# Attention key tiles: the odd 64 keys of two head pairs in one tile, and two pairs' sums in one PSUM bank

## The chip, the cores and the metric

One Trainium2 chip, one core. The metric is the device time of one execution in microseconds. The kernel before took 1009.11 us, the median of three runs (1012.57, 1009.09, 1009.11). One more execution, of 1010.09 us, was profiled.

## What is computed

Three layers in one kernel, all fp32. The change touches only the first.

```
# 1. random-feature attention: q, k, v of (4 batches, 8 heads, 576 positions, 64)
phi(x) = exp(h - max(h)) / sqrt(128),  h = x @ omega.T - sum(x*x)/2       # 128 features
kv  = sum over keys of phi(k)^T v        # (b, h, 128, 64)
z   = sum over keys of phi(k)            # (b, h, 128)
out = (phi(q) @ kv) / (phi(q) @ z + 1e-6)
# 2. x: (2304 tokens, 512) -> RMS norm -> silu(x w_gate) * (x w_val) -> w_out, d_ff 1536
# 3. 8 experts, capacity 288 each, greedy assignment by logits, relu(x w1) w2
```

576 keys are four tiles of 128 and a rest of 64.

## The kernel before, in words

**Layout.** The host lays k out as `kT[b, p]`, for pair p of heads (four pairs): 128 partitions are two heads by 64 dimensions, and 640 columns are the keys, the last 64 of them zero. `v1[b, p]` holds, for each of five tiles of 128 keys, both heads' values with a column of ones behind them (65 columns), zero where there is no key. The column of ones makes z come out with kv.

**Items.** Attention is a list of items. A `KItem(b, p, g)` takes key tiles 2g and 2g+1 of a pair; g = 2 has tile 4 only. A `QItem(b, t, hf)` takes 128 or 64 query rows and half of the heads. Per batch there are 12 key items and 10 query items, 88 in all. The loop over `tick` runs a new item in each tick, with six stages ("lags") of items overlapping.

A key item in lag 0 projects its tiles onto the features (for batch 0 by one fp32 matmul per tile, line 371; for the others by three fp32r matmuls of split operands, lines 366 to 368), takes the negated maximum (DVE, line 375) and two exponentials per tile (ACT, line 378). In lag 1 it multiplies the features with the values into a PSUM tile `pm` (line 412), which collects a pair's sums over its five tiles; after the last, ACT copies the 130 columns into `kvs` (line 422). For batches 1 to 3 the keys are split ahead of that (ACT line 341, GpSimd line 342). An fp32 matmul leaves two rows in the trace.

PSUM: `pm` has three banks, shared by the sums over keys and by three tiles of a query item; `pp` (projections) two, `gv` (feed-forward) two, `lg` one.

**Loads.** `load_k` (lines 332 and 333) is called three items ahead of a pair's first key item, on SP's queue, into tiles `kt` and `vt` of two buffers each; batch 0 is loaded at the start into rooms of another pool. SP's queue also carries the weights (line 518), queries (353) and stores (612).

**What runs beside attention.** Weights of layer 2 come as 64-bit words; 36 conversion units (24 of w_gate and w_val, 12 of w_out) turn them into fp32 with an ACT operation and three of DVE each (lines 526 to 528). They start at a rate of 0.3 per tick up to tick `FFN_AT` = 23, then two per tick until the first 24 are out, then 0.5 per tick. Feed-forward steps (24 fp32r matmuls each, lines 595 to 597, then ACT and DVE, lines 606 to 620) run one per tick, two in the dense ticks, as soon as a block of 256 tokens and its weights are there; from the third block on a step also waits for a unit of w_out. When a query item needs a fourth block, steps are run in a burst until one is free. Attention's instructions are traced with a raised priority (`AHEAD_A`), and a scheduler orders each engine's queue by priority and readiness. Behind attention, the rest of the feed-forward steps, the second half of layer 2 with the routing (a hand-written order) and the experts follow.

The start flag clears a whole bank's accumulation state, so only the first matmul into a `pm` tile sets it:

```
pk = st["pk", b, p]
for i, t in enumerate(self.ts):
    for h in range(2):
        nc.tensor.matmul(pk[:, h * (D + 1):(h + 1) * (D + 1)], self.ft[:, 2 * i + h, :], vt[:, t, h, :],
                         start=(t == 0 and h == 0), stop=(t == 4), skip_group_check=True)
```

Of the kernel before, what the change touches and what calls it, by code (L numbers as in the profile page):

```python
# [9 lines left out]
F32 = mybir.dt.float32  # L10
# [9 lines left out]
B, H, S, D, M = 4, 8, 576, 64, 128  # L20
# [21 lines left out]
EARLY = 6  # L42
SUB = 1
PACE = (0.3, 1.0, 0.5)
FFN_AT = 23
AHEAD_A = 200
HB = 6
LATE = 2
# [5 lines left out]
def const_f32():  # L54
    c = np.zeros((128, C_N), np.float32)
    i = np.arange(128)
    c[:, C_ID:C_SL] = np.eye(128)
    c[:, C_SL:C_SA] = np.arange(SL)
    c[:, C_SA:C_C] = np.arange(NSL)
    c[:, C_C:C_P] = np.arange(NC)  # L60
    c[:, C_P] = i
    c[:, C_E:C_T] = np.arange(E)
    e = np.arange(E)
    c[:, C_T:C_N] = (e[None, :] < e[:, None]).reshape(-1)
    return c


def triangles():
    i = np.arange(128)
    j = np.tile(np.arange(CAP), (128, 1))  # L70
    return np.concatenate([i[:, None] < i[None, :], i[:, None] >= i[None, :], j], 1).astype(np.float32)


def const_i32():
    rows = []
    for n, (d, s) in enumerate(zip(DIGITS, SHIFTS)):
        j = np.arange(1 if n else 2, 1 << d, dtype=np.uint32) << np.uint32(s)
        if n == 0:
            j = np.where(j >= 0x80000000, j ^ np.uint32(0x80000000), ~j)
        rows.append(j.astype(np.uint32))  # L80
    return np.tile(np.concatenate(rows).view(np.int32), (128, 1))
# [198 lines left out]
def kernel(ctx, tc, qT, kT, v1, om, wgv, rms, wo, wg2, w1, w2, cfd, trd, cid, out, dbg=None):  # L280
    nc = tc.nc
# [31 lines left out]
    kq = ac.enter_context(tc.tile_pool(name="kq", bufs=2))  # L313
    at = ac.enter_context(tc.tile_pool(name="at", bufs=2))
    psA = ac.enter_context(tc.tile_pool(name="psA", bufs=1, space=PSUM))

    st = {}


    kts, vts, khs, kvs, qhs = {}, {}, {}, {}, {}  # L320
    xblk, ready = {}, []

    def load_k(b, p):
        if b == 0:

            room = wpool.tile([128, 2, 1024], F32, name="wc")
            kt = room[:, 0, :640]
            vt = room[:, 1, :10 * (D + 1)].rearrange("p (t h d) -> p t h d", t=5, h=2)
        else:
            kt = kq.tile([128, 640], F32, name="kt")  # L330
            vt = kq.tile([128, 5, 2, D + 1], F32, name="vt")
        nc.sync.dma_start(kt, kT[b, p])
        nc.sync.dma_start(vt, v1[b, p])
        kts[b, p], vts[b, p] = kt, vt

    def split_k(b, p, g):
# [28 lines left out]
    def proj(pp, xh, xl):  # L365
        nc.tensor.matmul(pp, xh, omh, start=True, stop=False)
        nc.tensor.matmul(pp, xh, oml, start=False, stop=False)
        nc.tensor.matmul(pp, xl, omh, start=False, stop=True)  # L368

    def proj_whole(pp, x):  # L370
        nc.tensor.matmul(pp, x, oms, start=True, stop=True)

    def feat(pp, n, ng):
        mx = at.tile([128, 4], F32, name="mx")
        nc.vector.tensor_reduce(out=mx[:n, :ng], in_=pp[:n, :ng], axis=AX.X, op=OP.max, negate=True)  # L375
        ft = at.tile([128, 4, M], F32, name="ft", bufs=3)
        for g in range(ng):
            nc.scalar.activation(ft[:n, g], pp[:n, g], AF.Exp, bias=mx[:n, g:g + 1])  # L378
        return ft

    class KItem:
        def __init__(self, b, p, g):
            self.b, self.p, self.g = b, p, g
            self.ts = [t for t in (2 * g, 2 * g + 1) if t < 5]

        def load(self):
            if self.g == 0 and self.b:
                load_k(self.b, self.p)
# [5 lines left out]
        def pe(self, lag):  # L394
            b, p, g = self.b, self.p, self.g
            if lag == 0:
                self.pp = psA.tile([128, 4, M], F32, name="pp", bufs=2)
                if b == 0:
                    for i, t in enumerate(self.ts):
                        proj_whole(self.pp[:, 2 * i:2 * i + 2, :], kts[b, p][:, t * 128:t * 128 + 128])  # L400
                    return
                kh, kl = khs.pop((b, p, g))
                for i, t in enumerate(self.ts):
                    proj(self.pp[:, 2 * i:2 * i + 2, :], kh[:, i * 128:i * 128 + 128], kl[:, i * 128:i * 128 + 128])
            elif lag == 1:
                if g == 0:
                    st["pk", b, p] = psA.tile([128, 512], F32, name="pm", bufs=3)
                pk = st["pk", b, p]
                vt = vts[b, p]
                for i, t in enumerate(self.ts):  # L410
                    for h in range(2):
                        nc.tensor.matmul(pk[:, h * (D + 1):(h + 1) * (D + 1)], self.ft[:, 2 * i + h, :], vt[:, t, h, :],  # L412
                                         start=(t == 0 and h == 0), stop=(t == 4), skip_group_check=True)

        def el(self, lag):
            b, p, g = self.b, self.p, self.g
            if lag == 0:
                self.ft = feat(self.pp, 128, 2 * len(self.ts))
            elif lag == 1 and g == 2:
                if p == 0:  # L420
                    kvs[b] = at.tile([128, H, D + 1], F32, name="kvs")
                nc.scalar.copy(kvs[b][:, 2 * p:2 * p + 2, :].rearrange("p h d -> p (h d)"),
                               st.pop(("pk", b, p))[:, :2 * (D + 1)])

    class QItem:
        def __init__(self, b, t, hf):
# [262 lines left out]
    def ffn_step_el():  # L689
        if "el" in fst:  # L690
            j, f, pg = fst.pop("el")
            ffn_el(j, f, pg)
            ffn_rank_el()
            return j, f
        return None


    items = []
    for b in range(B):
        items += [KItem(b, p, g) for p in range(4) for g in range(3)]  # L700
        items += [QItem(b, t, hf) for t in range(5) for hf in range(2)]
    useq = [WgvUnit(f, g) for f in range(KF) for g in range(2)] + [WoUnit(f) for f in range(KF)]
    AHEAD = 3
# [1 line left out]
    ws = stage.tile([128, 2 * M], F32, name="ws")  # L705
    nc.scalar.dma_start(ws, om)
    load_k(0, 0)
    oms = wpool.tile([128, 2 * M], F32, name="wc")
    nc.scalar.mul(oms, ws, SCALE)
# [20 lines left out]
    def conv_pe(pace):  # L730
        conv["due"] += pace
        conv["live"] = [(lag + 1, u) for lag, u in conv["live"] if lag < 3]
        while conv["due"] >= 1 and conv["next"] < len(useq):
            conv["due"] -= 1
            conv["live"].append((0, useq[conv["next"]]))
            conv["next"] += 1
        for lag, u in conv["live"]:
            u.pe(lag)
# [8 lines left out]
    for tick in range(len(items) + NLAG - 1):  # L747
        live = [(lag, items[tick - lag]) for lag in range(NLAG) if 0 <= tick - lag < len(items)]
        conv_pe(PACE[0] if tick < FFN_AT else PACE[1] if conv["next"] < 2 * KF else PACE[2])
        with tc.high_priority(offset=AHEAD_A):  # L750
# [18 lines left out]
        ffn_step_el()  # L769
        if tick >= FFN_AT and conv["next"] < 2 * KF:  # L770
            for r in range(SUB):
# [268 lines left out]
def layouts(q, k, v, omega, moe_w_gate, moe_w_val, moe_w_out, moe_rms_g, moe2_w_gate, moe2_w1, moe2_w2):  # L1040
    a = np.asarray
    hp = H // 2

    def bits(x):
        return np.ascontiguousarray(x).view(np.int64)

    qT = a(q).reshape(B, hp, 2, S, D).transpose(0, 2, 4, 1, 3).reshape(B, 128, hp, S)
    kT = np.zeros((B, hp, 128, 640), np.float32)
    kT[..., :S] = a(k).reshape(B, hp, 2, S, D).transpose(0, 1, 2, 4, 3).reshape(B, hp, 128, S)
    v1 = np.zeros((B, hp, 2, 640, D + 1), np.float32)  # L1050
    v1[:, :, :, :S, :D] = a(v).reshape(B, hp, 2, S, D)
    v1[:, :, :, :S, D] = 1.0
    v1 = v1.reshape(B, hp, 2, 5, 128, D + 1).transpose(0, 1, 4, 3, 2, 5)
    om = np.zeros((128, 2 * M), np.float32)
    om[:D, :M] = a(omega).T
    om[D:, M:] = a(omega).T
    wgv = np.stack([bits(moe_w_gate), bits(moe_w_val)], 0).reshape(2, KD, 128, KF, 128).transpose(3, 2, 1, 0, 4)
    wgv = wgv.reshape(KF, 128, 1024)
    rms = np.tile(a(moe_rms_g)[None], (128, 1))
    wo = bits(moe_w_out).reshape(KF, 128, DM)  # L1060
    wg2 = a(moe2_w_gate).reshape(KD, 128, E).transpose(1, 0, 2)
    w1 = a(moe2_w1).reshape(E, KD, 128, 4, 256).transpose(0, 3, 2, 1, 4).reshape(E, 4, 128, 1024)
    w2 = a(moe2_w2).reshape(E, KE, 128, KD, 128).transpose(0, 3, 2, 1, 4).reshape(E, 4, 128, 1024)
    d = dict(qT=qT, kT=kT, v1=v1, om=om, wgv=wgv, rms=rms, wo=wo, wg2=wg2, w1=w1, w2=w2,
             cf=const_f32(), tri=triangles(), ci=const_i32())
    return {n: np.ascontiguousarray(x) for n, x in d.items()}
# [17 lines left out]
```

## Time and profile before

| | us |
|---|---|
| median of three runs | 1009.11 |
| profiled execution | 1010.09 |
| its span in the profile | 1008.2 |
| PE busy | 971.8 |
| weight loads (PEld) busy | 886.8 |
| DVE busy | 534.5 |
| ACT busy | 399.8 |
| POOL (GpSimd) busy | 242.1 |

The span is the time between the first and the last instruction of the profiled execution. Busy time counts overlapping rows once; rows of PE overlap, since a matmul's row holds its latency. PEld rows are the weight loads, which run beside the matmuls. In the slices of the page a digit is the busy share of 25.2 us in tenths,. "idle <- X" names what ended the idle time before an instruction.

### The profile page before, as it was taken

How to read it: one execution, taken by the hardware profiler on the slowest of the kernel's cores; microseconds unless marked ns; L12 is line 12 of the kernel's file. 1: busy time of each engine (PE TensorE's matmuls, PEld its weight loads, DVE VectorE, ACT ScalarE, POOL GpSimd, SP SyncE). 2: the span in 40 equal slices, each digit the busy share in tenths (PEclk: the TensorE clock that was granted, in tenths of full speed). 3: DMA queues.
4: the chain of work that ended last, by engine and by line, in shares of the span. 5: the costliest groups of instructions: out<-in, count | busy, mean ns of one | idle time of the engine just before them, and what ended most of it. 6: DMA issues, size and time to landing. Idle time of an engine off the chain costs nothing.

```text
span 1008.2 us, 19316 instructions
## 1 busy us (share of the span) xinstructions
PE 971.8 (96%) x7649; PEld 886.8 (88%) x7649; DVE 534.5 (53%) x1239; ACT 399.8 (40%) x999; POOL 242.1 (24%) x325
## 2 busy tenths in 40 slices
PE   6998899999999999999999999999997999999996
PEld 5888899989989989999999777777776999999996
DVE  3779956544653344432234465555554656665531
ACT  4985546546654544332233100100003644444420
POOL 1345512233344222322223000000005121222111
PEclk7999999999999999999999999999998999999998
DMA  8436752366544211732224466655536755655400
GB/s 274 158 113 207 222 160 81 127 212 200 178 144 148 102 53 49 202 112 83 83 98 156 138 183 203 189 175 161 158 94 213 246 187 189 199 194 193 150 24 24
DMA packets 112074, 153.32 MB, mean 152 GB/s; under 512 B 8560, under 2 KB 78832, under 8 KB 111984
## 3 DMA queue, kind: packets, MB, share of 16 engines
q1 hardware_dynamic: 108768, 142.52, 43.8%
q0 software_dynamic: 3072, 9.44, 2.9%
q8 instruction: 60, 0.98, 0.4%
q14 instruction: 30, 0.25, 0.1%
q10 hardware_dynamic: 144, 0.13, 0.0%
HBM read 108.03 MB, written 44.04 MB: 151 GB/s over the span
## 4 chain that ended last, share of the span: by engine, by line
PE 77%; issue 9%; DVE 6%; DMA 2%; ACT 2%; POOL 2%; SPq 0%; POOLq 0%; DVEq 0%; ACTq 0%
PE py L880 16%; PE gv L595 10%; PE gv L596 9%; PE gv L597 9%; PE pm L457 3%; PE pm L412 2%; PE cnt L163 2%; PE ph L968 2%; PE py L978 2%; PE ph L970 2%; PE ph L969 2%; PE py L979 2%; PE py L980 2%; DVE dw L527 2%; PE pm L453 2%
## 5 line engine op out<-in xcount | busy, mean ns | idle before, releaser
L595 PE MATMUL gv<-xh,wc 128*128 128x256 f32 x864 | 253.5, 294 | 6.4 <-DVE hp L610 6.0
L596 PE MATMUL gv<-xl,wc 128*128 128x256 f32 x864 | 250.1, 289 | 0.0
L597 PE MATMUL gv<-xh,wc 128*128 128x256 f32 x864 | 249.7, 289 | 0.0
L880 PE MATMUL py<-wc,ht 128*128 128x512 f32 x648 | 175.9, 409 | 0.0
L595 PEld LDWEIGHTS gv<-xh,wc 128*128 128x128 f32 x864 | 165.1, 191 | 10.7 <-DVE hp L610 7.0
L596 PEld LDWEIGHTS gv<-xl,wc 128*128 128x128 f32 x864 | 165.4, 191 | 0.8
L597 PEld LDWEIGHTS gv<-xh,wc 128*128 128x128 f32 x864 | 165.4, 191 | 0.6
L880 PEld LDWEIGHTS py<-wc,ht 128*128 128x128 f32 x648 | 114.4, 188 | 21.9
L607 DVE SCALAR_TENSOR_TENSOR th<-th,gv 128x256 f32<-128x256 f32 x108 | 45.1, 418 | 122.6 <-ACT th L606 122.4
L378 ACT ACTIVATE ft<-pp,mx 128x128 f32<-128x128 f32 (+1 forms) x320 | 93.9, 373 | 25.9 <-DVE mx L375 24.7
L620 POOL TENSOR_TENSOR hp<-h,hp 128x256 fp32r<-128x256 f32 x84 | 65.5, 780 | 156.1 <-ACT hp L619 156.0
L862 DVE TENSOR_TENSOR wc<-ws,wc 128x1024 fp32r<-128x1024 f32 x58 | 70.9, 1224 | 32.7 <-ACT wc L861 32.4
L606 ACT ACTIVATE th<-gv 128x256 f32<-128x256 f32 x108 | 41.5, 384 | 105.3 <-PE gv L597 105.0
L968 PE MATMUL ph<-exh,wc 128*128 128x288 f32 x256 | 78.9, 309 | 0.0
L978 PE MATMUL py<-ehh,wc 128*128 128x288 f32 x256 | 78.0, 305 | 0.0
L970 PE MATMUL ph<-exh,wc 128*128 128x288 f32 x256 | 76.2, 298 | 0.0
L969 PE MATMUL ph<-exl,wc 128*128 128x288 f32 x256 | 76.1, 298 | 0.0
L979 PE MATMUL py<-ehl,wc 128*128 128x288 f32 x256 | 75.9, 297 | 0.0
L980 PE MATMUL py<-ehh,wc 128*128 128x288 f32 x256 | 75.8, 296 | 0.0
L375 DVE TENSOR_REDUCE mx<-pp 128x4 f32<-128x512 f32 (+2 forms) x88 | 55.6, 635 | 33.9 <-PE pp L368 21.1
L889 ACT COPY ws<-py 128x512 f32<-128x512 f32 x18 | 10.6, 586 | 145.8 <-PE py L880 132.2
L861 ACT CAST wc<-ws 128x1024 fp32r<-128x1024 f32 x58 | 61.0, 1051 | 3.1 <-DMA ws<-in_w_dram 3.0
(197 smaller groups left out, 1843.2 us busy)
## 6 DMA issues: line engine op xcount, KB each, us to landing
ws<-in_w_dram SPq DMA_DIRECT2D x64, 512.0 KB, 3.4
ht<-h_dr SPq DMA_DIRECT2D x54, 512.0 KB, 4.2
h_dr<-hp SPq DMA_DIRECT2D x42, 512.0 KB, 2.6
ws<-in_wgv_dram SPq DMA_DIRECT2D x24, 512.0 KB, 4.0
ws<-in_wo_dram SPq DMA_DIRECT2D x12, 512.0 KB, 4.3
h_dr<-dw SPq DMA_DIRECT2D x24, 256.0 KB, 2.1
y_dr<-ws SPq DMA_DIRECT2D x18, 256.0 KB, 4.3
vt<-in_v_dram SPq DMA_DIRECT2D x12, 325.0 KB, 4.0
```

What stands on the lines that cost most here:

```text
L378: nc.scalar.activation(ft[:n, g], pp[:n, g], AF.Exp, bias=mx[:n, g:g + 1])
L595: nc.tensor.matmul(pg[:, v], w[:, 0, k, v], xh[:, k], start=(k == 0), stop=False)
L596: nc.tensor.matmul(pg[:, v], w[:, 0, k, v], xl[:, k], start=False, stop=False)
L597: nc.tensor.matmul(pg[:, v], w[:, 1, k, v], xh[:, k], start=False, stop=(k == KD - 1))
L862: lo.tensor_sub(w[:, 1], sv, w[:, 0])
L880: nc.tensor.matmul(py, ht[:, i4, a], w[:, l, f % 2], start=(f == 0 and n == 0), stop=(f == KF - 1 and n == 2))
L968: nc.tensor.matmul(ph, w[:, 0, k, m], xh[:, k], start=(k == 0), stop=False)
L969: nc.tensor.matmul(ph, w[:, 0, k, m], xl[:, k], start=False, stop=False)
L970: nc.tensor.matmul(ph, w[:, 1, k, m], xh[:, k], start=False, stop=(k == KD - 1))
L978: nc.tensor.matmul(py, w[:, 0, k], hh[:, k], start=(k == 0), stop=False)
L979: nc.tensor.matmul(py, w[:, 0, k], hl[:, k], start=False, stop=False)
L980: nc.tensor.matmul(py, w[:, 1, k], hh[:, k], start=False, stop=(k == KE - 1))
```

## The change

The last 64 keys of pairs 0 and 1, and of pairs 2 and 3, share one tile of 128 columns, stored as tile 4 of the odd pair: columns 512 to 575 are the even pair's keys, 576 to 639 the odd pair's. The odd pair's value tile has six entries instead of five: entry 4 holds the even pair's 64 rows and zeros below, entry 5 zeros and the odd pair's rows. For tile 4 the features are multiplied with both entries. Even pairs load 512 keys and four entries. The sums of two pairs (four heads by 65 columns) stand in one `pm` tile and are copied once, behind the odd pair's last item. The even pair has two items, the odd pair three: 10 key items per batch, 80 items in all. `FFN_AT` goes from 23 to 21.

```diff
-FFN_AT = 23
+FFN_AT = 21
 # load_k
-            vt = room[:, 1, :10 * (D + 1)].rearrange("p (t h d) -> p t h d", t=5, h=2)
+            vt = room[:, 1, :12 * (D + 1)].rearrange("p (t h d) -> p t h d", t=6, h=2)
-            vt = kq.tile([128, 5, 2, D + 1], F32, name="vt")
-        nc.sync.dma_start(kt, kT[b, p])
-        nc.sync.dma_start(vt, v1[b, p])
+            vt = kq.tile([128, 6, 2, D + 1], F32, name="vt")
+        n, m = (640, 6) if p % 2 else (512, 4)
+        nc.sync.dma_start(kt[:, :n], kT[b, p, :, :n])
+        nc.sync.dma_start(vt[:, :m], v1[b, p, :, :m])
 # KItem.pe, lag 1
-                if g == 0:
-                    st["pk", b, p] = psA.tile([128, 512], F32, name="pm", bufs=3)
-                pk = st["pk", b, p]
+                if g == 0 and p % 2 == 0:
+                    st["pk", b, p // 2] = psA.tile([128, 512], F32, name="pm", bufs=3)
+                pk = st["pk", b, p // 2][:, :4 * (D + 1)].rearrange("p (i h d) -> p i h d", i=2, h=2)
                 for i, t in enumerate(self.ts):
-                    for h in range(2):
-                        nc.tensor.matmul(pk[:, h * (D + 1):(h + 1) * (D + 1)], self.ft[:, 2 * i + h, :], vt[:, t, h, :],
-                                         start=(t == 0 and h == 0), stop=(t == 4), skip_group_check=True)
+                    for pair, tv in ((p % 2, t),) if t < 4 else ((0, 4), (1, 5)):
+                        for h in range(2):
+                            nc.tensor.matmul(pk[:, pair, h], self.ft[:, 2 * i + h, :], vt[:, tv, h, :],
+                                             start=(pair == 0 and t == 0 and h == 0), stop=(t == 4),
+                                             skip_group_check=True)
 # KItem.el, lag 1, g == 2
-                if p == 0:
+                if p == 1:
                     kvs[b] = at.tile([128, H, D + 1], F32, name="kvs")
-                nc.scalar.copy(kvs[b][:, 2 * p:2 * p + 2, :].rearrange("p h d -> p (h d)"),
-                               st.pop(("pk", b, p))[:, :2 * (D + 1)])
+                nc.scalar.copy(kvs[b][:, 2 * p - 2:2 * p + 2, :].rearrange("p h d -> p (h d)"),
+                               st.pop(("pk", b, p // 2))[:, :4 * (D + 1)])
 # the list of items
-        items += [KItem(b, p, g) for p in range(4) for g in range(3)]
+        items += [KItem(b, p, g) for p in range(4) for g in range(2 + p % 2)]
```

The host's layout of kT and v1 changes to match.

## Rows read from the trace of the kernel before

**Rows 1.** The page's busy shares, and the PE line of its 40 slices.
```profile
span 1008.2 us, 19316 instructions
PE 971.8 (96%) x7649; PEld 886.8 (88%) x7649; DVE 534.5 (53%) x1239; ACT 399.8 (40%) x999; POOL 242.1 (24%) x325
...
PE   6998899999999999999999999999997999999996
```

**Rows 2.** Busy time of each engine, in us with the count of rows, in stages cut by hand; then the granted clock, the DMA engines' share and GB/s.
```profile
13.00:35.00 22.00, 21.58 (x112) 19.73 (x113) 13.61 (x23) 15.47 (x49) 4.88 (x4) 0.78 0.62 203
35.00:60.00 25.00, 22.77 (x147) 18.02 (x146) 19.84 (x46) 21.53 (x66) 11.13 (x13) 1.00 0.49 156
...
71.00:117.00 46.00, 40.11 (x315) 38.72 (x313) 44.39 (x69) 26.88 (x68) 26.00 (x22) 0.96 0.65 208
...
128.00:412.00 284.00, 281.07 (x2325) 267.96 (x2324) 139.80 (x354) 148.27 (x443) 90.22 (x132) 1.00 0.42 136
```

**Rows 3.** The chain of waits that ended last in the window 0 to 140 us, in order of time: start, duration, what.
```profile
13.30 2.93 PE pp L371 x6
...
25.22 0.49 PE pp L371 x2
27.33 0.84 PE pm L412 x8
```

**Rows 4.** The same chain, further on.
```profile
77.19 1.35 DVE dw L528
...
87.09 1.68 DVE dw L527
```

**Rows 5.** Who waited for whom from 71 to 117 us, PE alone: us in total, times, longest.
```profile
PE gv L595 <- DVE hp L610: 4.9, 3, 2.1
```

**Rows 6.** Line 412 (the sums over keys): its rows in three windows around the second batch (PE busy and count, PEld busy and count), then its groups over the whole span, and line 422 (the copy): its group, with nothing listed under those who waited for it.
```profile
56.00:71.00 15.00, 3.14 (x22) 2.85 (x22) 1.00 0.37 111
71.00:117.00 46.00, 6.17 (x38) 5.79 (x38) 0.96 0.65 208
117.00:131.00 14.00, 3.30 (x20) 3.08 (x20) 1.00 0.74 245
...
L412 PE MATMUL pm<-vt,ft x240: 217/274/325, 63.9 to 350.4; 128*128 128x65 f32 x120
L412 PE MATMUL pm<-wc,ft x80: 220/275/452, 11.8 to 35.2; 128*128 128x65 f32 x80
...
L422 ACT COPY kvs<-pm x16: 243/268/292, 20.8 to 350.7; 128x130 f32<-128x130 f32 x16
...
who waited for it (us, times):
```

**Rows 7.** Groups by shape from 0 to 480 us: busy us and mean ns of one, then idle time before them.
```profile
L378 ACT ACTIVATE ft<-pp,mx 128x128 f32<-128x128 f32 x288 | 84.5, 374 | 21.8 <-DVE mx L375 20.5 <-DVE dn L478 0.6
L375 DVE TENSOR_REDUCE mx<-pp 128x4 f32<-128x512 f32 x64 | 43.5, 684 | 17.9 <-PE pp L368 9.4 <-PE pp L371 8.1
L375 DVE TENSOR_REDUCE mx<-pp 128x2 f32<-128x256 f32 x16 | 6.7, 421 | 16.0 <-PE pp L368 11.7 <-PE pp L371 4.3
L422 ACT COPY kvs<-pm 128x130 f32<-128x130 f32 x16 | 4.3, 268 | 6.8 <-PE pm L412 6.8
L470 ACT COPY qp<-pm 128x256 f32<-128x256 f32 x8 | 3.0, 372 | 6.7 <-PE pm L453 6.6
```

**Rows 8.** The timeline of PE at a key item of the second batch: start, duration, instruction.
```profile
56.22 0.28 PE L367 MATMUL pp<-oml,kh 128*128 128x256 f32 x1
...
56.58 0.28 PE L367 MATMUL pp<-oml,kh 128*128 128x256 f32 x1
```

**Rows 9.** Line 595 alone (one of the three lines of a feed-forward step) in two windows, then all rows in the same two: 160 to 170 us, in the second batch's queries, and 440 to 460 us, behind attention.
```profile
160.00:170.00 10.00, 1.90 (x6) 1.14 (x6) 1.00 0.15 41
...
440.00:460.00 20.00, 14.45 (x51) 9.66 (x51) 1.00 0.25 101
...
160.00:170.00 10.00, 10.00 (x87) 9.58 (x85) 5.76 (x17) 6.61 (x22) 2.79 (x6) 1.00 0.15 41
...
440.00:460.00 20.00, 20.00 (x168) 19.57 (x167) 7.82 (x20) 5.96 (x17) 5.27 (x8) 1.00 0.25 101
```

**Rows 10.** SP's queue: the load of the second batch's fourth value tile, and the times from issue to landing of all value tiles; ACT: the second batch's last three copies of sums.
```profile
86.61 0.38 SPq L333 DMA_DIRECT2D vt<-in_v_dram  x1
...
DMA to landing us min/median/max: 2.7/4.2/7.4
...
86.68 0.26 ACT L422 COPY kvs<-pm 128x130 f32<-128x130 f32 x1
113.44 0.24 ACT L422 COPY kvs<-pm 128x130 f32<-128x130 f32 x1
129.97 0.27 ACT L422 COPY kvs<-pm 128x130 f32<-128x130 f32 x1 [2.22 <-PE pm L412]
```

**Rows 11.** Busy time in stretches of 2 us at the start (columns as in rows 2); the number behind POOL's count is the granted clock.
```profile
8.00:10.00 2.00, 0.97 (x3) 0.25 (x1) 1.12 (x2) 0.67 (x1) 0.00 (x0) 1.00 1.04 399
10.00:12.00 2.00, 0.25 (x2) 0.25 (x2) 1.89 (x3) 0.67 (x3) 0.00 (x0) 1.00 1.03 414
...
20.00:22.00 2.00, 2.00 (x11) 1.91 (x10) 0.69 (x1) 1.15 (x4) 0.29 (x1) 0.50 0.65 260
...
24.00:26.00 2.00, 2.00 (x14) 1.82 (x14) 1.28 (x3) 1.10 (x4) 0.00 (x0) 1.00 0.00 0
```

More of the change, by code (lines that the diff above doesn't have):

```diff
@@ L1047, in layouts @@
     qT = a(q).reshape(B, hp, 2, S, D).transpose(0, 2, 4, 1, 3).reshape(B, 128, hp, S)
+    kt = a(k).reshape(B, hp, 2, S, D).transpose(0, 1, 2, 4, 3).reshape(B, hp, 128, S)
     kT = np.zeros((B, hp, 128, 640), np.float32)
[L1049 to L1053, printed above, removed]
+    kT[..., :512] = kt[..., :512]
+    kT[:, 1::2, :, 512:576] = kt[:, 0::2, :, 512:]
+    kT[:, 1::2, :, 576:] = kt[:, 1::2, :, 512:]
+    vo = np.ones((B, hp, 2, S, D + 1), np.float32)
+    vo[..., :D] = a(v).reshape(B, hp, 2, S, D)
+    v1 = np.zeros((B, hp, 128, 6, 2, D + 1), np.float32)
+    v1[:, :, :, :4] = vo[:, :, :, :512].reshape(B, hp, 2, 4, 128, D + 1).transpose(0, 1, 4, 3, 2, 5)
+    vo = vo[:, :, :, 512:].transpose(0, 1, 3, 2, 4)
+    v1[:, 1::2, :64, 4] = vo[:, 0::2]
+    v1[:, 1::2, 64:, 5] = vo[:, 1::2]
     om = np.zeros((128, 2 * M), np.float32)
```

## The prediction

> **What bounds the kernel now.** I read the page first: its busy shares and its 40 slices. The tensor engine (PE) counts as busy 96% of the span, and the PE row is full from the sixth slice on, but for one slice near 770 us and the last [rows 1]. The reader is to see that up to the end of attention, at 412 us, only the first five slices (126 us) show room. The change touches attention only. So I cut that part into stages by hand and read busy time per engine in each [rows 2]. From 13 to 35 us PE is busy 21.6 of 22 us (first batch, sums over keys). From 35 to 60 us PE, ScalarE (ACT) and VectorE (DVE) are all at 80 to 90%. From 71 to 117 us DVE is at 44.4 of 46 us and PE idles for 5.9 us: here the weights' words are converted. From 128 to 412 us PE shows almost no idle time.
>
> The chain of waits says the same by instruction: from 13 to 28 us it alternates between the projections (line 371) and the sums (line 412), both PE [rows 3]; from 76 to 91 us it holds DVE rows and short issue gaps, mostly lines 526 to 528 [rows 4]. In that stage PE's one large wait is for DVE: 4.9 us [rows 5].
>
> **The change, part by part.** Per batch there are 16 full key tiles and 4 half empty ones; now 16 and 2 filled from two pairs. With 4 batches, 8 of the 88 items and 8 projections of a tile go. The products of line 412 do not get fewer: the shared tile runs four where two tiles ran two each, so 320 rows stay [rows 6].
>
> First batch. A projection is one fp32 matmul, two rows. One of the two that go lies in the stretch at half clock, where six rows took 2.93 us, so 0.98 us for two; the other lies at full clock, where two rows take 0.49 us [rows 3]. Both stand on a chain of PE rows: **-1.5 us**. The ACT and DVE work that goes with them (two exponentials of about 0.37 us and one reduce of 0.42 us per tile [rows 7]) lies beside PE there. Without that cover they would be worth 0.75 us of ACT and 0.42 of DVE per tile more.
>
> Second batch. Its keys run through the stage that DVE bounds. The order in which the work is written there stays: by 117 us line 412 had issued 60 of its 80 rows [rows 6], nine items of twelve, and the projections stood one item further. With ten items, the same place in the order leaves only the last item's eight rows after 117 us. Prices: a fp32 row of line 412 takes 0.84/8 = 0.105 us [rows 3], a fp32r projection row 0.12 us, three of them 0.36 by their starts [rows 8]. Left over before: 20 rows of sums and three tiles of projections, 2.1 + 1.1 = 3.2 us. Left over after: 0.84 us. PE has room for what moves forward (1.6 us against 5.9 idle), so **-2.3 us** behind the stage. The stage itself gets one more full item in place of a light one: a reduce of 0.68 instead of 0.42 us on DVE [rows 7]: **+0.3 us**.
>
> Third and fourth batch. Four tiles of three rows at 0.12 us: **-1.4 us**, on a PE without idle time. Their casts, subtractions, reduces and exponentials go too, on engines half busy there [rows 2]; I cost them at nothing, and PE is what hides them.
>
> Gaps. PE "busy" hides that a row's latency overlaps the next. Weight loads are the finer measure: 19.57 of 20 us in the stretch 440 to 460 us that runs feed-forward steps alone [rows 9], but 268.0 of 284 us from 128 to 412 us [rows 2]. At the dense share that would be 278, so 10 us are lost in gaps over some 54 items, 0.185 us each. For the four items that go in the last two batches: **-0.7 us**. The bounds are 0 (gaps belong to the feed-forward work) and -1.6 (gaps come only with key items); I take the mean over items, because nothing in the waits ties them to one kind.
>
> The Trainium skill, in Perfetto Trace Analysis, Identifying the Most-Contended Engine, says that matmul busy time is a poor measure of how close TensorE is to its limit and that weight-load busy is the one to use. The trace agrees: PE shows 281.07 of 284 us where weight loads show 267.96 [rows 2]. By matmul busy, which leaves 2.9 us idle from 128 to 412 us, the term would be -0.2 and the sum -5.1.
>
> The copy. 16 copies of 130 columns at 0.27 us become 8 of 260, near the 0.37 us of a 256-column copy [rows 7]. No instruction on PE's queue is shown waiting for one [rows 6], and the next sum has two other banks. I cost it at zero; bounds -1.3 us (ACT time saved where ACT matters) and +3.0 (eight copies in PE's way).
>
> Loads. Even pairs move 20% less of both tensors, odd pairs 20% more of the values. Total bytes of v stay, those of k fall by a tenth. In the first 20 us DMA engines are full, but from 13 us on the chain holds no DMA; zero, bounds -0.4 and +0.4 us (a tenth of a landing of 4.2 us). One wait is new: the value tile of the fourth pair reuses the second pair's buffer, and with five items between them it is issued one item before that buffer's last use. On SP's queue what stands behind it (weight loads, stores) waits too. Before, the fourth pair's load was issued at 86.6 us, landings take 4.2 us, and its sums follow the third pair's copy at 113.4 us [rows 10]. One item there is some 9 us (three lie between the copies at 86.7 and 113.4), so the values would still land 13 us early. Zero; at most one landing of 4.2 us once per batch if the queue jams.
>
> FFN_AT moves from 23 to 21: in both kernels it falls on the second key item of the second batch, so conversion starts at the same work. Only the conversion units for wo shift: counted through the loop, the first comes one item behind the start of the second batch's queries instead of two ahead of it, and one earlier unit slides from a key item to a query item. Zero on the sum, and the source of a rival.
>
> **Sum.** -1.5 - 2.3 + 0.3 - 1.4 - 0.7 = -5.6 us. The profiled execution took 1010.09 us (span 1008.2), so 1004.5 on that footing; the median shown is 1.0 us lower, 1009.11, and from it I get **1003.5 us**. About 0.5% (5 us) is what a measurement of this kernel can tell from no change, so the forecast lies just beyond that line; with the bounds of gaps, copies' ACT time and loads it runs from 1001 to 1005.
>
> **Rivals.**
> *DVE keeps the gain.* If the end of the stage to 117 us is set by DVE's total alone, the first batch's 1.5 us only shrinks DVE's idle time: what counts is the two reduces less the one added, 0.84 - 0.27 = 0.6 us. If the key work finds no room there because PE stands in order behind the wait for line 610, only the 0.7 us that really go are won. -0.6 - 0.7 - 1.4 = -2.7: 1006.4 us. For it: [rows 4, 5]. Against it: the PE row has room in that stage, and key work is hoisted ahead of feed-forward work.
>
> *The clock stage moves.* From 12 to 22 us the granted clock is 0.5, the 1.2 GHz level, after PE had been busy only 1.2 of 4 us; from 24 us it is 1.00 [rows 11]. Ten us at half clock cost about 5 us. The pause comes from the first reduce standing behind conversion words on DVE. Another order there could spare it: 1003.5 - 5 = 998.5 us. Against it: the first two items and their loads keep their order.
>
> *Feed-forward steps run dry (slower).* Steps of the third block wait, in the order as written, for wo units, which come by item and not by work. Counting both loops, the old order has four empty items in a row (39 to 42) and two single ones; the new one has two empty and then five alternate items (48 to 56) without a step, and makes them up in one burst of six. A step is 24 rows at 0.119 us (168 rows in 20 us [rows 9]), 2.9 us. If PE stands idle for each of the five: +14.3, **1017.8 us**. It passes the line for slower once about four of the five gaps stay open (10.6 us lost). Against it: from 160 to 170 us PE ran only a quarter of its usual feed-forward rows, 6 against some 25 per 10 us, and still held 9.58 us of weight loads [rows 9]; attention fills such a hole by itself.
>
> *The joint copy gets in PE's way.* Two pairs now share one bank for five items, so a sum cannot start in another bank while the first is copied. If each of the eight copies held PE up for 0.37 us: +3.0, 1006.5 us. Against it [rows 6]. The Trainium skill, in Perfetto Trace Analysis, Matmuls, advises that independent matmul groups rotate through different banks so that evacuating one overlaps the next; by it this edit would cost that time, and no row here shows such a wait.
>
> *Nothing comes of it:* the removed items were filled by waiting work anyway: 1009.1 us.
>
> **How the numbers follow.** Forecast 0.50, of which 0.36 beyond the line and 0.14 short of it; DVE keeps the gain 0.22; clock 0.10; copy 0.05; steps run dry 0.09; nothing 0.04. Faster: 0.36 + 0.10 = 0.46. Same: 0.14 + 0.22 + 0.05 + 0.04 = 0.45. Slower: 0.09. The range 998 to 1009.5 takes in every case but the dry steps and the outer half of the clock case, 0.14 left out.
>
> **What would show it.** Right: line 371 loses four rows and lines 366 to 368 eighteen together; line 412 keeps 320; the copy appears 8 times near 0.37 us; the second batch's last copy comes right behind the conversion stage, 10 us or so earlier than 130 us; attention ends some 5 us earlier and everything behind it is only shifted. Wrong: the stage that DVE bounds is longer by what the first batch won; PE waits for line 422 or for the value tile; weight-load share falls between 170 and 270 us; the stretch at half clock has another length; or the routing stage behind 590 us changes its length, which nothing here argues for.

## The result, and the profile after

The changed kernel took 1019.86 us (median of 6 runs, 1013.89 to 1021.77) where the kernel before took 1009.15 us in the same rounds (1007.99 to 1012.57): ratio 1.0092, 95% interval 1.0064 to 1.0121. It is 0.9% slower. The forecast of 1003.5 us and the range up to 1009.5 both missed; the time is near that of the rival "feed-forward steps run dry" (1017.8 us), which had been given a chance of 0.09. The profiled execution took 1017.93 us.

The page of the changed kernel, its busy shares and the PE and clock lines of the slices (compare [rows 1]):
```profile
span 1016.1 us, 19192 instructions
PE 976.9 (96%) x7627; PEld 891.7 (88%) x7627; DVE 534.0 (53%) x1231; ACT 392.3 (39%) x969; POOL 242.3 (24%) x319
...
PE   6998999999899999999999999999996999999996
...
PEclk8999999999989999999999999999998999999999
```
The 22 rows fewer are the four of line 371 and the eighteen of lines 366 to 368 that were announced. But a digit in the PE line and one in the clock line now fall under 9 in the two slices from 254 to 305 us, in the middle of attention, where the kernel before shows 9 in both lines.

The four stages of [rows 2], in the changed kernel:
```profile
13.00:35.00 22.00, 21.07 (x118) 18.33 (x117) 15.58 (x24) 16.75 (x51) 8.64 (x7) 0.87 0.73 234
35.00:60.00 25.00, 24.17 (x169) 20.17 (x169) 22.56 (x52) 22.49 (x67) 10.50 (x14) 1.00 0.48 155
71.00:117.00 46.00, 40.32 (x322) 39.50 (x320) 44.90 (x68) 26.30 (x62) 25.61 (x19) 0.96 0.63 212
128.00:412.00 284.00, 277.64 (x2236) 265.01 (x2236) 132.39 (x337) 139.56 (x412) 87.47 (x125) 0.98 0.39 127
```
The first three stages hold more rows than before (118 against 112, 169 against 147, 322 against 315): work moved forward, as forecast. (In the first stage a shorter stretch at half clock helps, 0.87 against 0.78; more on it below.) From 128 to 412 us there are 89 rows fewer than before, PE is idle 3.4 us longer, and the granted clock is 0.98 instead of 1.00. Cut into 40 us, all rows, the kernel before:
```profile
200.00:240.00 40.00, 37.80 (x318) 36.56 (x318) 19.39 (x42) 20.97 (x58) 15.16 (x20) 1.00 0.64 210
240.00:280.00 40.00, 39.88 (x340) 38.32 (x340) 22.96 (x61) 25.19 (x72) 14.05 (x19) 1.00 0.53 172
280.00:320.00 40.00, 40.00 (x319) 36.51 (x318) 18.04 (x46) 20.45 (x63) 19.23 (x31) 1.00 0.44 154
```
and the changed kernel:
```profile
200.00:240.00 40.00, 39.88 (x339) 38.76 (x338) 19.21 (x45) 21.38 (x64) 16.21 (x19) 1.00 0.59 195
240.00:280.00 40.00, 35.69 (x286) 33.56 (x286) 24.69 (x63) 23.66 (x70) 15.18 (x22) 0.96 0.40 131
280.00:320.00 40.00, 39.25 (x292) 37.84 (x293) 14.64 (x39) 18.16 (x55) 14.40 (x23) 0.87 0.44 152
```
The loss sits in the two windows from 240 to 320 us: 54 and 27 rows fewer than before. The kernel before is not without such places either: it idles 2.2 us from 200 to 240 us, but its granted clock stays at 1.00 there. What is missing is read from one of the three lines of a feed-forward step alone (columns: PE and PEld busy with counts, clock, DMA), before:
```profile
240.00:280.00 40.00, 13.71 (x48) 9.09 (x48) 1.00 0.53 172
280.00:320.00 40.00, 17.03 (x57) 10.73 (x57) 1.00 0.44 154
320.00:360.00 40.00, 18.90 (x66) 12.24 (x65) 1.00 0.27 92
```
and after:
```profile
240.00:280.00 40.00, 7.48 (x24) 5.00 (x24) 0.96 0.40 131
280.00:320.00 40.00, 16.29 (x54) 11.10 (x55) 0.87 0.44 152
320.00:360.00 40.00, 21.73 (x75) 14.19 (x75) 1.00 0.43 151
```
A line has 8 rows per step: three steps instead of six from 240 to 280 us, and about one of the missing ones has come by 360 us. This fits the alternate items without a step and the burst behind them that the rival counted out of the loops. Below, a hole is a stretch in which feed-forward rows are missing and PE idles. The chain of waits that ended last goes there through the store of a conversion unit of w_out (start, duration, what):
```profile
242.70 4.39 DMA wo_dr<-dw
```
Finer, all rows of the changed kernel in stretches of 4 us, inside the hole and behind it:
```profile
240.00:244.00 4.00, 3.96 (x35) 3.88 (x36) 4.00 (x10) 3.69 (x12) 2.25 (x3) 1.00 0.50 159
244.00:248.00 4.00, 3.00 (x27) 2.86 (x25) 0.10 (x1) 1.23 (x4) 1.46 (x2) 1.00 0.83 277
...
252.00:256.00 4.00, 2.58 (x24) 2.23 (x21) 2.47 (x6) 4.00 (x13) 2.34 (x4) 1.00 0.27 66
256.00:260.00 4.00, 3.51 (x21) 3.54 (x22) 2.65 (x7) 1.75 (x6) 0.00 (x0) 0.69 0.56 179
```
```profile
284.00:288.00 4.00, 3.25 (x30) 2.98 (x30) 2.06 (x7) 2.48 (x7) 0.62 (x1) 1.00 0.51 190
288.00:292.00 4.00, 4.00 (x23) 3.72 (x22) 1.31 (x3) 1.20 (x3) 1.52 (x3) 0.53 0.11 33
292.00:296.00 4.00, 4.00 (x25) 4.00 (x24) 3.15 (x6) 3.80 (x14) 2.29 (x4) 0.62 0.78 270
296.00:300.00 4.00, 4.00 (x37) 3.80 (x35) 1.57 (x3) 2.55 (x9) 0.68 (x2) 1.00 0.72 229
```
Both places cost twice. First PE stands idle (1.4 of 4 us from 252 us). Then the granted clock falls to the 1.2 GHz level: from 288 to 292 us PE counts as busy all the time and issues 23 rows where 37 go at full clock. Not every hole has this second part. In the kernel before PE was busy 2.96 of 4 us and went on at full clock:
```profile
200.00:204.00 4.00, 2.96 (x24) 2.63 (x24) 3.25 (x8) 2.30 (x6) 1.52 (x2) 1.00 0.32 95
204.00:208.00 4.00, 4.00 (x37) 4.00 (x36) 0.83 (x2) 3.03 (x10) 0.92 (x2) 1.00 0.81 273
```

To weigh the parts I took every row of PE's timeline up to the last feed-forward row at its full-clock price (0.1165 us for a feed-forward or projection row, 0.105 us for a row of sums or products), counted half of every stretch at half clock as lost, and called the rest idle. After less before: work -2.6, half clock +5.1 (6.8 more from 240 to 320 us, by the clock columns above, and 1.7 less at the start), idle +3.1, together +5.6: the last feed-forward row starts at 561.1 instead of 555.5 us. The remaining 2.3 us of the span's +7.9 lie behind it; from 760 to 800 us, where both kernels pause, the granted clock is 0.87 instead of 0.91, which is an estimated 1.6 us of them. All this is one execution of each kernel.

### The profile page after: what moved, and what is told of

The parts are those of the page before. It is cut to its first block, busy times and chain, and to the rows that moved or that the text cites. A ratio compares the mean times of both kernels' runs of the same rounds, so it can differ in the third digit from the quotient of the medians.

```text
span 1016.1 us, 19192 instructions
## 1 busy us (share of the span) xinstructions
PE 976.9 (96%) x7627; PEld 891.7 (88%) x7627; DVE 534.0 (53%) x1231; ACT 392.3 (39%) x969; POOL 242.3 (24%) x319
## 4 chain that ended last, share of the span: by engine, by line
PE 75%; issue 9%; DVE 6%; DMA 4%; ACT 2%; POOL 2%; SPq 0%; POOLq 0%; ACTq 0%; DVEq 0%
PE py L885 16%; PE gv L600 9%; PE gv L601 9%; PE gv L602 9%; PE pm L462 2%; PE cnt L163 2%; PE ph L973 2%; PE ph L975 2%; PE ph L974 2%; PE py L983 2%; PE py L984 2%; PE py L985 2%; PE pm L416 2%; DVE dw L532 2%; PE pm L458 2%
## 5 line engine op out<-in xcount | busy, mean ns | idle before, releaser
L379 ACT ACTIVATE ft<-pp,mx 128x128 f32<-128x128 f32 (+1 forms) x304 | 88.8, 373 | 38.6 <-DVE mx L376 38.1
L624 ACT CAST hp<-h 128x256 fp32r<-128x256 f32 x84 | 34.1, 406 | 66.3 <-DVE h L623 65.9
```

## The experiments

All were timed in five rounds beside the kernel before, whose median there was 1010.4 to 1011.8 us (1009.15 beside the changed kernel). A ratio compares a kernel with the kernel before in the same rounds; medians from different rounds can differ by 1 to 3 us for that reason alone. "Rate" is the third number of PACE, the conversion units of w_out per tick.

**Feeding the changed kernel earlier.**
```
-PACE = (0.3, 1.0, 0.5)
+PACE = (0.3, 1.0, 0.7)    # in the changed kernel
```


> The changed kernel with the third rate of conversion at 0.7 units per item instead of 0.5, so that counted through the loop no feed-forward step of blocks 3 and 4 waits for a unit of w_out (five waited in the changed kernel, two in the kernel before). Theory A (steps run dry): the loss between 240 and 320 us goes and the gain of the removed tiles stays, 1001 to 1007 us. Theory B (the joint copy or the shared bank holds PE): no change, 1017 to 1021. Theory C (clock, by chance of the order): anything between, with half-clock stretches as long as before.

Measured: 1012.29 us (1007.28 to 1018.26), ratio 1.0020 [1.0000, 1.0041]. Between the two: 7.6 us less than the changed kernel, so the units' timing carries most of the loss; but not the 1001 to 1007 of theory A.

**Starving the kernel before.**
```
-PACE = (0.3, 1.0, 0.5)
+PACE = (0.3, 1.0, 0.45)   # in the kernel before
```


> The kernel before with that rate at 0.45 instead of 0.5: counted through the loop four steps wait for units of w_out instead of two, with a burst of two behind them. Nothing of the key tiles is changed. Theory A: 3 to 8 us slower than before, 1012 to 1017, with a dry stretch about 240 to 290 us. Theory B: as before, 1008 to 1011.

Measured: 1008.41 us, ratio 0.9976 [0.9962, 0.9991]. Theory A missed: later units made the kernel before a little faster. The place where PE idles 2.2 us has only moved, from 200 to 240 us to 240 to 280 us, and the granted clock stays at 1.00 in both. The number of steps that wait, counted in the loops, does not give the size of a loss.

**The joint bank and copy alone.** The kernel before, its tiles apart, the sums of two pairs in one bank and one copy:
```
-if g == 0:
+if g == 0 and p % 2 == 0:
...
-elif lag == 1 and g == 2:
+elif lag == 1 and g == 2 and p % 2:
...
-nc.scalar.copy(kvs[b][:, 2 * p:2 * p + 2, :]...
+nc.scalar.copy(kvs[b][:, 2 * p - 2:2 * p + 2, :]...
```


> The kernel before with two pairs' sums in one bank and one copy, but twelve key items and all tiles as before. Theory A: no difference, 1007 to 1011. Theory B: most of the loss is here, 1013 or more, and PE waits for the copy or for a bank of pm.

Measured: 1010.34 us, ratio 1.0001 [0.9981, 1.0021]: theory A. Within 2 us, this half of the change costs and gives nothing.

**The higher rate alone.** Rate 0.7 in the kernel before (the same line as in the first experiment).

> The kernel before with the rate at 0.7. Control for the first run. Theory A: the two waiting steps of the kernel before go, worth little since it shows no dry stretch: 1004 to 1010, and in any case a smaller gain than the first run shows against the changed kernel. If the rate itself is what pays, the gain is as large as in the first run, 13 us or more.

Measured: 1018.78 us, ratio 1.0079 [1.0060, 1.0098]. Neither expectation held: the higher rate is no gain here but a loss. The kernel before can be made about as slow as the changed one without touching its tiles. Its trace has a hole of its own: line 595 has no row from 192 to 208 us (all rows of PE):
```profile
200.00:204.00 4.00, 2.85 (x21) 2.33 (x20) 1.39 (x2) 2.14 (x7) 2.26 (x4) 1.00 0.80 282
204.00:208.00 4.00, 4.00 (x22) 4.00 (x22) 1.55 (x5) 2.68 (x9) 0.00 (x0) 0.57 0.42 149
208.00:212.00 4.00, 4.00 (x23) 4.00 (x23) 2.14 (x3) 1.73 (x7) 1.19 (x2) 0.58 0.17 34
```
The same two parts: 1.15 us of idle time, then 8 us at a granted clock of 0.57 and 0.58 with 45 rows instead of some 73. A hole in the feed-forward rows with half clock behind it is therefore no property of the shared tiles.

**Short query rows.** The first experiment's trace had few holes, yet little gain, so something else took time. The timeline of PE in the changed kernel, where the transposes (line 458) of a query tile of 64 rows run between feed-forward rows:
```profile
121.23 0.27 PE L458 MATMUL pm<-cf,ft 64*128 64x64 f32 x1
121.44 0.38 PE L601 MATMUL gv<-xl,wc 128*128 128x256 f32 x1
121.75 0.27 PE L458 MATMUL pm<-cf,ft 64*128 64x64 f32 x1
121.95 0.39 PE L602 MATMUL gv<-xh,wc 128*128 128x256 f32 x1
```
Read the starts: 0.31 us from a feed-forward row to a short row, 0.20 back, 0.52 us per pair. The next experiment works the 64-row tiles as 128 rows, the rest zeros from the host, on top of rate 0.7:
```
-        o, n = q_tiles(b)[t]
+        o, n = q_tiles(b)[t][0], 128
...
-            n, b, t, hf = self.n, self.b, self.t, self.hf
+            n, b, t, hf = 128, self.b, self.t, self.hf
...
+    qT = np.zeros((B, 128, hp, 640), np.float32)
+    qT[..., :S] = a(q).reshape(B, hp, 2, S, D)...
```


> The changed kernel with the rate at 0.7 (the first run's) and with query tiles of 64 rows worked as 128 rows through projection, features, transposes and products; the surplus rows are dropped at the end. The traces show that a fp32 row of a 64-row tile between two feed-forward rows costs 0.31 + 0.20 us from start to start, against 0.20 + 0.03 for a full one; such pairs number 51 in the first run's kernel, 41 in the changed kernel, 35 in the kernel before. Theory D (these pairs ate the first run's gain): some 6 to 12 us less than the first run, 1000 to 1006. Rival E (the cost is of the alternation itself, whatever the rows, or is hidden): within 2 us of the first run, 1010 to 1014.

Measured: **994.93 us** (993.77 to 1000.06), ratio 0.9850 [0.9825, 0.9875]; it beats both kernels, and by more than theory D had given it. Its timeline at such a place:
```profile
123.34 0.27 PE L458 MATMUL pm<-cf,ft 128*128 128x128 f32 x1
123.36 0.36 PE L602 MATMUL gv<-xl,wc 128*128 128x256 f32 x1
123.57 0.27 PE L458 MATMUL pm<-cf,ft 128*128 128x128 f32 x1
123.59 0.36 PE L603 MATMUL gv<-xh,wc 128*128 128x256 f32 x1
```
0.21 us to the fp32 row, 0.02 back, 0.23 us per pair: 128 columns instead of 64, in less than half the time. And the stretch that lost before is full (all rows):
```profile
240.00:280.00 40.00, 40.00 (x343) 39.11 (x342) 22.06 (x61) 22.55 (x65) 16.77 (x26) 1.00 0.45 158
280.00:320.00 40.00, 40.00 (x347) 39.34 (x346) 16.65 (x38) 22.21 (x71) 19.47 (x29) 1.00 0.47 164
```

**Full rows in the kernel before**, rate 0.5; the edit of the last experiment without its rate:
```
-        o, n = q_tiles(b)[t]
+        o, n = q_tiles(b)[t][0], 128    # in the kernel before
...
```


> The kernel before with query tiles of 64 rows worked as 128, nothing else. Theory D: 35 pairs by 0.29 us go, 5 to 10 us less, 1000 to 1006. Rival E: 1008 to 1012.

Measured: 1006.13 us, ratio 0.9942 [0.9923, 0.9962]: the direction of theory D, at the edge of its range.

**Full rows in the changed kernel**, rate 0.5, the same edit.

> The changed kernel with query tiles of 64 rows worked as 128, the rate left at 0.5. Theory D with the dry stretch: 5 to 12 us less than the changed kernel's 1020, 1008 to 1015, and the thin stretch about 250 to 300 us with its half clock still there; the gap to the fifth run (the same with the rate at 0.7) is what the dry stretch costs, 5 to 9 us. If the dry stretch was harmless, no gap.

Measured: 1006.57 us, ratio 0.9958 [0.9938, 0.9978], just below the range expected. The hole is still there (all rows):
```profile
240.00:280.00 40.00, 35.86 (x271) 33.95 (x271) 22.33 (x54) 23.39 (x68) 15.77 (x21) 0.91 0.39 127
280.00:320.00 40.00, 38.41 (x318) 36.71 (x318) 14.98 (x40) 17.64 (x52) 15.91 (x24) 1.00 0.50 174
```
101 rows fewer in these 80 us than at rate 0.7, and 11.6 us more in the time, where 5 to 9 had been expected.

**The shared tiles alone.** The changed kernel with a bank and a copy for each pair:
```
-                if g == 0 and p % 2 == 0:
+                if g == 0:
...
+                for o in (p - 1, p):
+                    nc.scalar.copy(kvs[b][:, 2 * o:2 * o + 2, :]...
```


> The changed kernel with a bank and a copy for each pair: the tiles and items are merged, the sums are not. Theory A (order of the steps, from the items): as the changed kernel, 1017 to 1021, with the same dry stretch. Theory B (joint bank or copy): most of the loss gone, 1004 to 1010.

Measured: 1017.38 us, ratio 1.0057 [1.0035, 1.0078]: theory A. The loss goes with the shared tiles and the shorter list of items, not with the bank.

**Rate 0.7 and full rows in the kernel before** (the edits of the fourth and fifth experiments, tiles apart).

> The kernel before with both edits of the fifth run: rate 0.7 and 64-row query tiles worked as 128. With the fifth, sixth and seventh run this makes a square of key tiles (separate or shared) by rate (0.5 or 0.7). If the rate pays by itself, 994 to 999, and the shared tiles are worth nothing. If it pays only where steps wait for w_out, it does not help here: 1004 to 1014, since the old order's four items in a row without a step stay and the fourth run (the rate alone) was 8 us slower than before; the shared tiles are then worth 10 us or more once the steps are fed.

Measured: 1009.66 us, ratio 0.9996 [0.9979, 1.0013]: the rate does not pay by itself. With tiles apart it takes away what the full rows gave.

**Rate 0.55 with full rows in the changed kernel.**
```
-PACE = (0.3, 1.0, 0.5)
+PACE = (0.3, 1.0, 0.55)   # and the full rows
```


> Dose: the seventh run's kernel (changed, 64-row tiles as 128) with the rate at 0.55, so that counted through the loop three steps wait for w_out and three are made up in a burst, against five and five at 0.5 (1006.6 us) and none at 0.7 (994.9). If the loss follows the number of waiting steps: 1000 to 1004. If it is a matter of chance in the order, anywhere from 994 to 1010.

Measured: 997.42 us (996.76 to 998.60), ratio 0.9879 [0.9861, 0.9897]. Below the expectation: nearly all of what 0.7 gives is there at 0.55.

**The start of conversion back at 23.**
```
-FFN_AT = 21
+FFN_AT = 23               # in the changed kernel
```


> One part undone: the changed kernel with FFN_AT back at 23, so that dense conversion starts two items later against the work. Counted through the loop six steps wait for w_out and six come in the burst. Dry theory: slower than the changed kernel by 1 to 6 us, 1020 to 1026. If the move to 21 is what hurts: 1009 to 1013.

Measured: 1015.91 us (1014.40 to 1017.01), ratio 1.0059 [1.0043, 1.0074]. A miss on both sides: more steps wait by count, and it is no slower than the changed kernel (its ratio's interval overlaps the changed kernel's, 1.0064 to 1.0121); nor does the move to 21 explain the loss. The hole is the same one, 293 and 288 rows where the changed kernel has 286 and 292:
```profile
240.00:280.00 40.00, 35.57 (x293) 33.71 (x291) 25.41 (x61) 23.64 (x71) 15.08 (x20) 0.96 0.45 151
280.00:320.00 40.00, 38.11 (x288) 35.65 (x288) 14.82 (x39) 16.95 (x52) 14.27 (x22) 0.91 0.41 145
```
The count of waiting steps finds the place and not the price.

**Rate 0.55 alone** (the line of the experiment with 0.55, without the full rows).

> The changed kernel with one number different: the third rate of conversion units per item is 0.55 instead of 0.5; query tiles of 64 rows stay as they are. Theory A (the loss sits in the items of the third and fourth batch in which no feed-forward row is ready, whatever the shape of the query rows): with the 128-row tiles this rate was worth 9.2 us (1006.6 to 997.4), so here 1019.9 - 9 = 1011, range 1007 to 1014; from 240 to 320 us the clock is lost for less than 2.5 us and PE counts at least 74 of 80 us busy. Theory B (the loss needs the 64-row tiles: short query rows next to feed-forward rows are the larger part and more even feeding only makes more of such pairs): 1015 to 1020, as with rate 0.5.

Measured: 1009.17 us (1005.32 to 1014.78), ratio 0.9997 [0.9978, 1.0015]: theory A. All rows:
```profile
240.00:280.00 40.00, 37.29 (x321) 35.74 (x320) 26.12 (x68) 26.90 (x77) 16.07 (x23) 1.00 0.51 165
280.00:320.00 40.00, 40.00 (x342) 38.80 (x341) 13.58 (x36) 16.98 (x53) 18.18 (x28) 1.00 0.48 168
```
85 rows more than in the changed kernel in the same 80 us, PE busy 77.3 of them, and no half clock there. From one line: the 0.05 more per tick is worth 10.7 us with short query rows (1019.86 to 1009.17) and 9.2 us with full ones (1006.57 to 997.42); by the ratios, which leave out the difference between rounds, 9.6 and 8.0 us.

The medians side by side, in us (from different rounds, see above):

| tiles, query rows | 0.45 | 0.5 | 0.55 | 0.7 |
|---|---|---|---|---|
| apart, 64 (kernel before) | 1008.4 | 1009.2 | | 1018.8 |
| shared, 64 (changed kernel) | | 1019.9 | 1009.2 | 1012.3 |
| apart, 128 | | 1006.1 | | 1009.7 |
| shared, 128 | | 1006.6 | 997.4 | 994.9 |

## Why the prediction was wrong, step by step

**First batch, -1.5 us: about as forecast, with some luck of the clock in the pair of profiles.** The second batch's sums start at 60.7 us instead of 63.9 [rows 6], but half clock lasted 6.8 us here from 12 us on and 10.2 us before, which is an estimated 1.7 of these 3.2 us. In the six profiles with query tiles of 64 rows and no half clock from 12 to 36 us they start at 60.0 to 60.5 us with shared tiles and at 61.4 to 61.7 with tiles apart: some 1.3 us. By 240 us PE had issued 1703 rows where the kernel before had issued 1679, and the ten rows that left the first two batches' lists come on top: 34 rows, some 4 us, ahead, again with that 1.7 in it.

**The clock stage moves, -5 us in a rival: it moved, but not by the change.** The stretch at half clock from 12 us on is shorter than before, as one sign of being wrong had it. It is absent from 13 to 35 us (granted clock 1.00) in the profiles of the kernel before at rates 0.45 and 0.7, whose first items are the same. So it differs from one execution to the next, and a pair of profiles can be 5 us apart by it.

**Second batch, -2.3 and +0.3 us: as forecast up to 118 us.** The last eight rows of the sums are all that is left behind the conversion stage (line 416 from 117 to 134 us), and the copy behind them comes at 118.32 us instead of 129.97 [rows 10]:
```profile
117.00:134.00 17.00, 1.25 (x8) 1.05 (x7) 1.00 0.69 236
```
```profile
118.32 0.38 ACT L427 COPY kvs<-pm 128x260 f32<-128x260 f32 x1 [0.51 <-PE pm L416]
```
The stage did not give it back: PE's wait there, 4.9 us in [rows 5], became
```profile
PE gv L600 <- DVE hp L615: 5.7, 4, 2.0
```
and the stage still took in seven rows more. "DVE keeps the gain" is not what this stage shows.

**Third and fourth batch, -1.4 us: there, but buried.** The full-price work fell by 2.6 us in all (22 rows), which holds these twelve rows.

**Gaps, -0.7 us: not found.** From 128 to 412 us idle time grew by 3.4 us. The term spread the lost time evenly over items; the rows above show it where feed-forward rows are missing and at short query rows.

**The copy, zero: right.**
```profile
L427 ACT COPY kvs<-pm x8: 360/380/400, 24.5 to 353.8; 128x260 f32<-128x260 f32 x8
```
Nobody is listed as waiting for it, line 416 keeps its 320 rows, and the experiment with the bank alone gave 1.0001. For the case that the rule of the Trainium skill, Perfetto Trace Analysis, Matmuls, to rotate independent groups through banks, decides here, the prediction had put down +3.0 us; the interval of this measurement ends at +2.1.

**Loads, zero: right.** The new wait is there: SP's queue stood behind the sums with a value tile's load (us in total, times, longest, from 60 to 140 us),
```profile
SPq L334 <- PE pm L416: 5.8, 2, 5.1
```
but in all of attention no instruction of PE is listed as waiting for a load.

**Conversion units of wo shift, "zero on the sum": the step that failed.** The place was right: the items without a step were counted from the loops ahead of the run, and the trace has the hole there. The argument against its price was wrong. It took one stretch, 160 to 170 us, where attention with a quarter of the usual feed-forward rows had held 9.58 us of weight loads [rows 9], and made a rule of it: "attention fills such a hole by itself". From 252 to 260 us attention did not fill it: 24 and 21 rows in 4 us where 37 is full, with the granted clock at 0.69 in the second. What PE waited for from 240 to 320 us (us in total, times, longest):
```profile
PE pm L458 <- DVE xl L504: 1.9, 1, 1.9
PE gv L575 <- ACT dw L585: 1.8, 2, 1.0
PE pm L416 <- ACT ft L379: 0.8, 2, 0.6
```
That is attention's own steps on DVE and ACT, and the conversion of w_out itself: the main work has waits of its own, and here no feed-forward rows stood ready to cover them. And behind the hole comes half clock, which stood in no term. In the pair of profiles the idle time grew by 3.1 us net and half clock by 5.1, where the rival had 14.3 us of idle time (five steps); measured by the rate alone, with short and with full rows, the hole costs 8 to 11 us. With its mechanism given 0.09, the chances were off; that the rival's 1017.8 us came so near is luck, since its price was one of idle time only.

**Short query rows: in no step at all.** Summed over the starts in PE's timeline from 40 to 555 us, rows next to a 64-row tile took beyond their price an estimated 9.6 us in the kernel before, 9.8 in the changed one, 9.9 at rate 0.55, 14.0 at rate 0.7 and 7.1 in the kernel before at rate 0.45. So they don't explain the changed kernel's loss. They do fit that rate 0.7 stops 3 us short of 0.55 in the changed kernel (+4.1 by the sum) and that 0.45 helped the kernel before (-2.5 by the sum, -2.4 measured): a feed-forward row that is ready at such a place makes a pair. The sums are of one profile each.

**What stays open.** With the steps fed, the changed kernel is level with the kernel before (0.9997) and not 5.6 us ahead. The clock takes part of the gain. Over the twelve executions at rate 0.55 the mean granted clock of an execution is 0.978 to 0.992, and the time follows it, from 1014.78 and 1014.13 us at 0.978 to 1005.32 at 0.992. Their mean clock is 0.9853, that of the seventeen executions of the kernel before beside them 0.9895. At the same clock, 0.984 to 0.986, six of them took 1008.15 to 1011.19 us and four of the kernel before 1011.83 to 1013.32: 2 to 3 us ahead. Why the changed kernel gets the lower clock was not settled. Nor was the clock's share of the loss at rate 0.5: of its six executions the three at 0.983 to 0.986 took 1019.63 to 1021.77 us, still some 8 us above the kernel before at 0.984 to 0.986, so over many executions the clock's share looks smaller than the 5.1 us of the two profiles. With 128-row tiles the shared tiles give 9 to 11 us between the best versions by the medians, 6 to 9 by the ratios, more than the forecast; the kernel before with full rows ran at two rates only, its best may lie between, and the split of that gain was not measured.

## What to carry to other kernels

Where filler work is released by count (so much per item) and the change takes items away, first write out which items get no filler, then look in the trace at what the main work does alone in just those items; one stretch that held up elsewhere is no bound. A hole of 1 to 2 us in TensorE's rows can cost several more through the clock, and need not: price it with and without half clock behind it. Compare the granted clock of many executions before reading a difference of a few us out of two profiles. Retune such a rate together with the change: the same edit costs 10.7 us or nothing by 0.05 in one constant, and 0.7, good for one order of items, costs 8 us in the other.

## What the runs showed of the hardware

- An fp32 row (here a transpose) and an fp32r feed-forward row that alternate took 0.52 us per pair where the fp32 row belongs to a 64-row tile, and 0.23 us where it belongs to a 128-row tile. Padding with zeros was the faster form.
- TensorE's records show a PE busy 4.00 of 4 us at half clock (288 to 292 us, granted clock 0.53, 23 rows); only the clock column and the count of rows tell it from a full stretch. The drop followed a stretch in which PE was busy 3.25 of 4 us; in the hole at 252 us it followed 2.58 of 4. In the kernel before, 2.96 of 4 us (from 200 us) was followed by 4 us at 1.00 with 37 rows.
- The twelve executions of one kernel (rate 0.55) ran at a mean granted clock of 0.978 to 0.992 and took 1014.78 to 1005.32 us, on the whole the slower the lower the clock.
- Four heads' sums in one bank and one copy of 260 columns (0.38 us) took the same time as two banks and two copies of 130 (0.27 us each): ratio 1.0001 [0.9981, 1.0021].
